# Additions of partial outputs: from VectorE to copies on ScalarE and accumulating transfers

## The chip, the cores and the metric

The kernel runs on one core of one Trainium2 chip. The metric is device microseconds of one execution. Before the change the median of three runs is 2104.79 us (2104.72 to 2105.66).

## The reference

For each of 4 batches with N = 6080 tokens and C = 256 channels, columns of q and k are normalised over the tokens, a 256x256 matrix of attention over channels is made, and v goes through it. The result, 24320 tokens in all, goes through a mixture layer with 2048 hidden columns:

```python
qn = q / (norm(q, axis=1) + 1e-06);  kn = k / (norm(k, axis=1) + 1e-06)
a = softmax(kn.transpose(0, 2, 1) @ qn / tau)
x = (v @ a).reshape(24320, 256)
h = x @ w_in
g = where(h >= 1, h, where(h <= -1, 0, (h + 1) ** 2 / 4))
out = g @ w_out
```

## The kernel before

The attention matrix is multiplied into w_in first, so that each batch has its own weights W = a @ w_in and the tokens of v meet W alone. Tokens run along the free dimension. A pair (`pairs`, index k) is two blocks of 512 tokens (480 in the last pair); a batch has 6 pairs. The 2048 hidden columns are 8 slices of 256 (index i). One group is (b, k, i); there are 4 x 6 x 8 = 192.

`h_ops` makes the four 128-row tiles of h of one group with seven products instead of eight (`strassen`, L1132), each product three matmuls of single-precision parts (`mm3`). ScalarE and VectorE turn a tile into g: saturation at L1327, square at L1331, maximum at L1336, and `operand` (L1339) splits g into a high part (L1346) and a low part (L1349). `o_ops` multiplies these by w_out into four output banks, O00 to O11, that are held for a whole pair.

For the first SPLIT[b][k] slices of a pair the output is made by `strassen_o` instead, with seven products per slice. There some products go to a bank directly, and sums of g (`combos`, L1394) go through the bank O01 in stages; ENDS gives how many stages a pair has (one for SPLIT 2 to 4, two for 5 and 6). SPLIT has 2, 2, 3, 4, 5, 5 for the pairs of the first batch, 5 throughout the next two, and 5, 5, 5, 5, 6, 6 for the last. Between stages the helper `into` reads the bank: the first time ScalarE copies it into a page in SBUF (L1438), and later times VectorE adds it to that page (L1440). At the end of a pair the four banks are read: where a page of partial sums exists VectorE adds the bank to it (L1484), and otherwise ScalarE copies the bank (L1487). SyncE then stores the page to DRAM (L1490).

The order of all work is made in Python before the program is built. `Order.op` records an operation with its engine, a cost, what it reads and writes, and a rank from the table ORDER, one number per operation; `Order.run` places the operations one after another, by rank among those that can start. It books engine times by `COST`, gives pages and banks out of pools, and for a transfer books its landing by AHEAD = 1.2, BYTES = 403e3, 1.3 us and a slack (STORE = 1.5 for stores to DRAM). Each engine then runs its own list in that order and waits on semaphores. SyncE begins the loads and stores: weights of the next groups (`load_W`, L824, two buffers in w_mem), tokens (L1265), stores (L1490). GpSimd begins loads that cast on the way (`cast_load`, L830) and does some of the subtractions.

Pages are 40 tiles of 128x512 words, those of kinds u, s, m and r among 28 of them. A page is free again when all that reads it is done.

Of the kernel before, what the change touches and what calls it, by code (L numbers as in the profile page):

```python
# [13 lines left out]
ALU = mybir.AluOpType  # L14
# [47 lines left out]
class Order:  # L62
# [20 lines left out]
    def cost(self, eng, dur, r):  # L83

        if isinstance(dur, float):
            return dur, dur, eng in self.OTHER
        kind, n, more = dur
        if kind == "dma":
            return 0.56, 0.56, False
        bank = any(x.pool and x.pool.bank for x in r)  # L90
        a, b, c = self.COST["actb" if kind == "act" and bank else kind]
        t = a + b * n + more
        return t, t + c, eng == "POOL" or eng == "DVE" and (kind == "dve1" or not bank)
# [166 lines left out]
def dve_us(n):  # L260
    return "dve", n, 0.0
# [29 lines left out]
STORE = 1.5  # L291
WOP_DUE = -48
GRAM_END = -1
CAST = 1.0
AT_ONCE = 4
# [385 lines left out]
def channel_attention_moe(ctx: ExitStack, tc: tile.TileContext, kq, kqT, vT, tau, w_in, w_out, outT):  # L681
# [132 lines left out]
    def page(kind):  # L814
        return Buf(pools["pg"], kind=kind)
# [569 lines left out]
    def combos(g, u):  # L1385
# [5 lines left out]
        for k_, out, a, c in ((0, c1, u[1, 1], u[1, 0]), (1, u[1, 0], u[1, 0], u[0, 0]), (2, c0, u[1, 1], u[1, 0]),  # L1391
# [7 lines left out]
            else:  # L1399
                op("POOL", pool_us(n), less(nc.gpsimd), r=[a, c], w=[out], due=due,  # L1400
                   other=[("DVE", dve_us(n), less(nc.vector), LATE["alt"][3])])

    def strassen_o(g):

        b, k, i = groups[g]
# [249 lines left out]
```

## Time and profile before

| | |
|---|---|
| median of three runs | 2104.79 us |
| the profiled execution | 2105.08 us |
| its span, first to last instruction | 2103.3 us |
| TensorE busy | 2090.9 us (99%) |
| VectorE busy | 1985.0 us (94%) |
| ScalarE busy | 1822.2 us (87%) |
| GpSimd busy | 896.6 us (43%) |
| granted TensorE clock | 1.00 |

Busy time is the union of the times in which an engine's instructions run. Ends of matmuls are modelled and overlap the next matmul's start, so a short idle time of TensorE is not drawn, and the steps between starts tell more.

### The profile page before, as it was taken

The numbers are of one execution on the slowest core, as the hardware profiler recorded it, in microseconds if no ns is written. First come the engines' busy times: TensorE is split into PE (matmuls) and PEld (weight loads), VectorE is DVE, ScalarE is ACT, GpSimd is POOL, SyncE is SP. The second block draws the span as 40 slices with busy tenths as digits, with TensorE's granted clock in tenths as the row PEclk, the third lists the DMA queues.
The fourth block names the chain that finished last, engine by engine and source line by source line (L and its number), as shares of the span: only waits on it lengthen the run. The fifth ranks groups of instructions, "written<-read, shape, count | busy, mean of one in ns | idle before, by whom it ended". The sixth has DMA issues, their size and how long they took to land. (4 is left out here: it accounts for less than half of the span.)

```text
span 2103.3 us, 30498 instructions
## 1 busy us (share of the span) xinstructions
PE 2090.9 (99%) x9535; PEld 1728.1 (82%) x9535; DVE 1985.0 (94%) x3165; ACT 1822.2 (87%) x3362; POOL 896.6 (43%) x953
## 2 busy tenths in 40 slices
PE   9999999999999999999999999999999999999999
PEld 7888888888878888888888888888788888788887
DVE  8898899999999999999999999999999999999998
ACT  6788889888898988888998888888999988988986
POOL 0234244544344655443435444544344443544442
PEclk9999999999999999999999999999999999999999
DMA  9865566654876866758657676675775434433432
GB/s 387 322 208 187 188 218 224 202 170 139 277 240 230 272 216 228 263 175 283 208 193 251 218 256 228 222 250 186 243 237 176 158 108 132 152 123 115 152 108 72
DMA packets 163202, 432.12 MB, mean 205 GB/s; under 512 B 22048, under 2 KB 59296, under 8 KB 160480
## 3 DMA queue, kind: packets, MB, share of 16 engines
q1 hardware_dynamic: 137744, 384.36, 52.7%
q0 software_dynamic: 25296, 45.82, 7.7%
q8 instruction: 75, 1.23, 0.2%
q14 instruction: 87, 0.71, 0.1%
HBM read 359.33 MB, written 70.78 MB: 204 GB/s over the span
## 5 line engine op out<-in xcount | busy, mean ns | idle before, releaser
L955 PE MATMUL bank<-v,w_mem 128*128 128x512 f32 (+1 forms) x3264 | 859.8, 391 | 5.1 <-DMA w_mem<-w_d 2.1
L955 PEld LDWEIGHTS bank<-v,w_mem 128*128 128x128 f32 x3264 | 603.8, 188 | 145.6 <-DVE bank L1139 8.4
L955 PE MATMUL bank<-p,wout 128*128 128x512 f32 (+1 forms) x1746 | 553.2, 388 | 0.4 <-DVE p L1349 0.4
L955 PE MATMUL bank<-x,wout 128*128 128x512 f32 (+1 forms) x1500 | 493.9, 388 | 0.0
L955 PEld LDWEIGHTS bank<-p,wout 128*128 128x128 f32 x1746 | 327.0, 188 | 67.8 <-DVE p L1349 1.3
L955 PEld LDWEIGHTS bank<-x,wout 128*128 128x128 f32 x1500 | 280.8, 188 | 57.6 <-DVE x L1349 0.5
L955 PE MATMUL bank<-x,w_mem 128*128 128x512 f32 (+1 forms) x768 | 214.8, 389 | 0.1
L955 PE MATMUL bank<-p,wsum 128*128 128x512 f32 (+1 forms) x579 | 190.1, 389 | 0.0
L955 PEld LDWEIGHTS bank<-x,w_mem 128*128 128x128 f32 x768 | 142.5, 188 | 32.0 <-ACT bank L1136 1.5
L1331 ACT ACTIVATE u_mem<-u_mem 128x512 f32<-128x512 f32 (+1 forms) x249 | 156.1, 630 | 3.5
L955 PE MATMUL bank<-x,wsum 128*128 128x512 f32 (+1 forms) x444 | 150.3, 388 | 0.0
L1331 ACT ACTIVATE p<-p 128x512 f32<-128x512 f32 (+1 forms) x229 | 144.0, 631 | 2.1
L1327 ACT ACTIVATE u_mem<-bank 128x512 f32<-128x512 f32 (+1 forms) x193 | 114.1, 592 | 29.1 <-PE bank L955 27.9
L955 PEld LDWEIGHTS bank<-p,wsum 128*128 128x128 f32 x579 | 108.0, 188 | 23.9 <-DVE p L1440 0.7
L1136 ACT COPY bank<-bank 128x512 f32<-128x512 f32 (+1 forms) x198 | 115.7, 585 | 4.6 <-PE bank L955 1.9
L1327 ACT ACTIVATE p<-bank 128x512 f32<-128x512 f32 (+1 forms) x175 | 103.1, 591 | 12.6 <-PE bank L955 11.5
L1287 DVE TENSOR_TENSOR v<-raw_mem,v 128x512 fp32r<-128x512 f32 (+1 forms) x136 | 103.6, 770 | 1.5 <-ACT v L1292 0.6
L1275 POOL TENSOR_TENSOR raw_mem<-raw_mem 128x512 f32<-128x512 f32 (+1 forms) x52 | 66.8, 1285 | 87.4 <-DVE p L1349 20.0
L1346 ACT CAST p<-p 128x512 fp32r<-128x512 f32 (+1 forms) x147 | 89.6, 614 | 13.4 <-DVE p L1336 8.1
L955 PEld LDWEIGHTS bank<-x,wsum 128*128 128x128 f32 x444 | 82.9, 188 | 17.4 <-DVE x L1349 0.4
L1336 DVE TENSOR_TENSOR u_mem<-bank,u_mem 128x512 f32<-128x512 f32 (+1 forms) x130 | 87.7, 675 | 6.3 <-ACT u_mem L1331 5.8
L1336 DVE TENSOR_TENSOR p<-bank,p 128x512 f32<-128x512 f32 (+1 forms) x133 | 89.5, 673 | 3.7 <-ACT p L1331 3.5
(519 smaller groups left out, 4619.5 us busy)
## 6 DMA issues: line engine op xcount, KB each, us to landing
w_mem<-w_d SPq DMA_DIRECT2D x176, 896.0 KB, 4.8
raw_mem<-kqT SPq DMA_DIRECT2D x60, 512.0 KB, 6.3
raw_mem<-kq SPq DMA_DIRECT2D x51, 512.0 KB, 5.8
kq<-kq SPq DMA_DIRECT2D x20, 1024.0 KB, 9.0
raw_mem<-vT SPq DMA_DIRECT2D x40, 512.0 KB, 6.6
p<-kq POOLq DMA_DIRECT2D x59, 256.0 KB, 5.8
w_d<-w_mem SPq DMA_DIRECT2D x16, 896.0 KB, 5.3
p<-wop_d SPq DMA_DIRECT2D x54, 256.0 KB, 5.2
```

The costliest lines, as they stand in the source:

```text
L955: nc.tensor.matmul(out, lhsT=lhs(a), rhs=rhs(c), start=start and m == 0, stop=stop and m == 2, skip_group_check=skip)
L1136: op("ACT", act_us(n), lambda: nc.scalar.copy(a.ap[:, :n], z.ap[:, :n]), r=[z], w=[a], due=early[1])
L1275: return lambda: e.tensor_tensor(out=part(o), in0=part(a), in1=part(c), op=ALU.subtract)
L1287: op("DVE", dve_us(n), lambda: nc.vector.tensor_tensor(out=vs[x].ap[:, 1, :n], in0=part(src), in1=f32(vs[x].ap[:, 0, :n]), op=ALU.subtract ...
L1327: op("ACT", act_us(n), lambda: nc.scalar.activation(u.ap[:, :n], h.ap[:, :n], IDENTITY_SAT240, scale=240.0), r=[h], w=[u], table="sat", du ...
L1331: op("ACT", act_us(n), lambda: nc.scalar.activation(u.ap[:, :n], u.ap[:, :n], AF.Square, bias=0.5, scale=1.0 / 480.0), r=[u], w=[u], due=due)
L1336: op("DVE", dve_us(n), lambda: nc.vector.tensor_tensor(out=out.ap[:, :n], in0=h.ap[:, :n], in1=u.ap[:, :n], op=ALU.max), r=[h, u], w=[out] ...
L1346: return lambda: f(t[0].ap[:, :n], src.ap[:, :n])
```

## The change

A new helper `add_out` stands where VectorE added a bank to a page, in `into` and at the end of a pair. Except in the very last pair, ScalarE copies the bank into a page of its own, and GpSimd begins a transfer that adds this page to the page of partial sums. Such a transfer is booked at 0.56 + 0.34 us on GpSimd in the order, and its landing with the slack STORE. ORDER has 168 more entries (11290 for 11122) and other numbers throughout.

```diff
         if kind == "dma":
-            return 0.56, 0.56, False
+            return 0.56 + more, 0.56 + more, False
...
 CAST = 1.0
+ADD = "dma", 0, 0.34
 AT_ONCE = 4
...
 ORDER = """
...
+    def add_out(bk, src, r, n, due):
+
+        if bk == (B - 1, KP - 1):
+            op("DVE", dve_us(n), lambda: nc.vector.tensor_tensor(
+                out=r.ap[:, :n], in0=src.ap[:, :n], in1=r.ap[:, :n], op=ALU.add), r=[src, r], w=[r], due=due)
+            return
+        t = page("r")
+        op("ACT", act_us(n), lambda: nc.scalar.copy(t.ap[:, :n], src.ap[:, :n]), r=[src], w=[t], due=due)
+        op("POOL", ADD, lambda: nc.gpsimd.dma_start(out=r.ap[:, :n], in_=t.ap[:, :n], accum_op=ALU.add), r=[t, r], w=[r],
+           due=due + 2, size=n * 512, slack=STORE)
+
     def strassen_o(g):
...
             else:
-                op("DVE", dve_us(n), lambda: nc.vector.tensor_tensor(
-                    out=r[x].ap[:, :n], in0=src.ap[:, :n], in1=r[x].ap[:, :n], op=ALU.add), r=[src, r[x]], w=[r[x]], due=due)
+                add_out((b, k), src, r[x], n, due)
...
                     if r:
-                        op("DVE", dve_us(n), lambda o=o, yb=yb: nc.vector.tensor_tensor(
-                           out=yb.ap[:, :n], in0=o.ap[:, :n], in1=yb.ap[:, :n], op=ALU.add), r=[o, yb], w=[yb], due=due)
+                        add_out((b, k), o, yb, n, due)
```

## Rows read from the trace of the kernel before

**Rows 1.** The page, part 1: busy us, share of the span, instructions.

```profile
PE 2090.9 (99%) x9535; PEld 1728.1 (82%) x9535; DVE 1985.0 (94%) x3165; ACT 1822.2 (87%) x3362; POOL 896.6 (43%) x953
```

**Rows 2.** Windows: length, busy us of PE, PEld, DVE, ACT, POOL; clock; DMA share; GB/s.

```profile
0.00:100.00 100.00, 97.26 (x453) 82.71 (x454) 83.28 (x128) 67.12 (x99) 11.27 (x26) 1.00 0.93 363
...
600.00:700.00 100.00, 97.78 (x462) 79.83 (x461) 96.90 (x153) 89.59 (x165) 48.44 (x61) 1.00 0.75 249
...
sum 2100.00, PE 2090.94 PEld 1728.09 DVE 1984.98 ACT 1822.22 POOL 896.55; mean PE 99.57 PEld 82.29 DVE 94.52 ACT 86.77 POOL 42.69
```

**Rows 3.** Timeline of TensorE: start, us, what, count [idle before <- releaser].

```profile
1843.29 2.88 PE L955 MATMUL bank<-v,w_mem 128*128 128x512 f32 x12
```

**Rows 4.** Timeline of TensorE: first, largest and last stalls from 100 us on.

```profile
359.64 1.63 PE L955 MATMUL bank<-v,w_mem 128*128 128x512 f32 x6 [1.04 <-DMA w_mem<-w_d]
...
626.12 0.96 PE L955 MATMUL bank<-v,w_mem 128*128 128x512 f32 x3 [1.62 <-DVE bank L1139]
...
1742.78 0.93 PE L955 MATMUL bank<-v,w_mem 128*128 128x512 f32 x3 [0.74 <-DMA w_mem<-w_d]
...
1837.03 0.97 PE L955 MATMUL bank<-v,w_mem 128*128 128x512 f32 x3
```

**Rows 5.** Waits of weight loads: who waited for whom: us, times, longest.

```profile
PEld bank L955 <- DVE bank L1139: 9.7, 27, 2.0
PEld bank L955 <- ACT bank L1136: 6.2, 20, 0.8
```

**Rows 6.** Lines L1440, L1484, L1438: ns min/median/max, first and last start, forms.

```profile
L1440 DVE TENSOR_TENSOR p<-bank,p x33: 637/676/692, 118.3 to 2080.7; 128x512 f32<-128x512 f32 x24, 128x480 f32<-128x480 f32 x9
...
L1484 DVE TENSOR_TENSOR p<-bank,p x39: 641/676/692, 184.5 to 2098.1; 128x512 f32<-128x512 f32 x32, 128x480 f32<-128x480 f32 x7
...
L1438 ACT COPY p<-bank x39: 539/579/618, 99.9 to 2054.5; 128x512 f32<-128x512 f32 x32, 128x480 f32<-128x480 f32 x7
```

**Rows 7.** Timeline of VectorE before the stall at 626.12.

```profile
607.43 0.65 DVE L1484 TENSOR_TENSOR p<-bank,p 128x480 f32<-128x480 f32 x1
...
624.78 0.68 DVE L1394 TENSOR_TENSOR p<-c,u_mem 128x512 f32<-128x512 f32 x1
625.38 0.68 DVE L1139 TENSOR_TENSOR bank<-bank,p 128x512 f32<-128x512 f32 x1
```

**Rows 8.** Timeline of ScalarE in the same stretch.

```profile
622.19 0.59 ACT L1136 COPY bank<-bank 128x512 f32<-128x512 f32 x1
622.70 0.60 ACT L1327 ACTIVATE mh_mem<-bank 128x512 f32<-128x512 f32 x1
```

**Rows 9.** Line L830: ns min/median/max of the issues, and their landings.

```profile
L830 POOL DMA_DIRECT2D p<-kq x62: 514/547/577, 148.0 to 1409.3; - x62
...
DMA to landing us min/median/max: 2.7/5.9/13.2
```

**Rows 10.** The page, part 5: busy us, mean ns of one | idle before, releaser.

```profile
L1275 POOL TENSOR_TENSOR raw_mem<-raw_mem 128x512 f32<-128x512 f32 (+1 forms) x52 | 66.8, 1285 | 87.4 <-DVE p L1349 20.0
```

**Rows 11.** DMA: queue with packets, MB, share; issues with KB, us to landing.

```profile
q0 software_dynamic: 25296, 45.82, 7.7%
...
w_mem<-w_d SPq DMA_DIRECT2D x176, 896.0 KB, 4.8
...
outT<-u_mem SPq DMA_DIRECT2D x21, 256.0 KB, 2.1
```

**Rows 12.** Timeline of SyncE: start and length of the issues.

```profile
181.38 0.32 SPq L824 DMA_DIRECT2D w_mem<-w_d  x1
...
1733.86 0.33 SPq L1490 DMA_DIRECT2D outT<-p  x1
1734.29 0.69 SPq L824 DMA_DIRECT2D w_mem<-w_d  x1
...
2044.11 0.33 SPq L824 DMA_DIRECT2D w_mem<-w_d  x1
```

**Rows 13.** Waits of SyncE: us in total, times, longest.

```profile
SPq L1490 <- DVE p L1484: 133.3, 36, 9.6
```

609 rows, old and new, of the table ORDER are left out of this document.

## The prediction

> **What bounds the kernel now.** I read the page's first part, then the windows of 100 us, the timeline of TensorE, the waits, and last the two lines that change and the queues around them. TensorE is the bound: 2090.9 of 2103.3 us busy, against 1985.0 for VectorE, 1822.2 for ScalarE and 896.6 for GpSimd [rows 1]. The windows tell how little is left. Their sum has TensorE busy 2090.94 of 2100 us, and the first window alone lacks 2.74, so 6.3 us of visible idle time lie behind it; window 600:700 holds a third of that, 2.2, with VectorE at 96.9 [rows 2]. Twelve unbroken matmuls take 2.88 us and one is drawn 0.39 long [rows 3], so the pace is (2.88 - 0.39) / 11 = 0.226 us a matmul, and each drawn idle time is a loss larger by 0.39 - 0.226 = 0.165.
>
> From 100 us on I count 22 steps of the TensorE timeline that exceed the pace by over 0.13 us, from the one that ends at 359.64 to the one that ends at 1837.03 [rows 4]. 6.3 + 22 x 0.165 = 9.9, less about 0.6 behind the last matmul, and the steps themselves give 9.2. By what ended them: VectorE 13 times, 5.0 us, of which 1.8 at 626.12 alone; weights from DRAM 3 times, 2.6 us; ScalarE 6 times, 1.5 us. The waits of weight loads show the same makers in the same order, partly hidden in the queue: VectorE's L1139 9.7 us, ScalarE's L1136 6.2 [rows 5]. So 9.2 us, 0.44% of the time, is what any relief of VectorE or ScalarE can bring; all else is matmuls that the change leaves alone. The granted clock is 1.00, the upper level of 2.4 GHz, in every window.
>
> **What it removes.** The additions of L1440 and L1484 take 0.68 us each [rows 6]. By SPLIT and ENDS a pair of one stage has 4 of them and a pair of two stages 8; 4 pairs are of the first kind and 20 of the second, 176 in all, and the last pair's 8 stay, so 168 go. VectorE's starts stand 0.60 us apart where it runs unbroken (624.78 to 625.38) [rows 7], so it gets back 168 x 0.60 = 101 us; its busy time falls to about 1884.
>
> What that is worth is read where TensorE stood. Behind 10 of the 13 stalls that VectorE ended, its unbroken run (no gap over 0.15 us) contains one or more of the additions; the largest, at 626.12, follows a run that has L1484 at 607.43 in it and four additions in all [rows 4, 7]: 4 x 0.60 = 2.4 us earlier against 1.8 us of stall. These ten sum to 3.8 us. I take -3.8; the ends are 0 (the order of after puts other work into the place) and -5.0 (all thirteen go).
>
> **What it adds to ScalarE.** 168 copies out of a bank of 0.58 us, as L1438 makes them already, with the next start 0.51 behind a copy in an unbroken run [rows 6, 8]. 168 x 0.51 = 86 us, so ScalarE goes from 1822 to 1908, and its idle time from 281 to 195. That idle time is the cover; where it is gone, copies at L1136 and squares come later, and TensorE waits for both. The six ScalarE stalls, 1.5 us, grow in my estimate as idle time shrinks: x 281/195, +0.7. Ends: -1.5 (better placed), and +5.3, if each new copy costs TensorE as much as each of the 198 at L1136 makes weight loads wait: 6.2 / 198 x 168.
>
> The bank itself comes free from a copy instead of an addition, 0.58 for 0.68 us: no cost, unless the copy stands late in ScalarE's order.
>
> **What it adds to GpSimd.** 168 issues. The nearest are the cast loads at L830: 514 to 577 ns in their largest group [rows 9]. None there accumulates; the code itself books 0.90 for one. So 168 x 0.55 = 92 us, with ends of 86 (0.514) and 216 (1.285, GpSimd's full subtraction [rows 10]): 896.6 becomes 983 to 1113 of 2103. Its idle time hides this. But each issue waits in GpSimd's order for ScalarE's copy, and on a page with two additions for the landing of the first; behind it stand L1349's and L1394's operands, which TensorE needs. I take 0 for that, since over 980 us stay idle, and price its failure below.
>
> **What it adds to the transfers.** 168 of at most 256 KB are 43 MB, about what queue 0 moves now in 7.7% of the engines' time [rows 11]: +7%, or +14% if reading the sum's own page counts as much again. In window 600:700 the engines are at 75% [rows 2], so they don't become the bound.
>
> **What it moves: the stores.** A store to outT now waits for an addition of 0.68 us; afterwards it waits for copy, issue and landing. SyncE takes its queue in order, so what stands behind a waiting store waits with it. 33 of the 96 stores have the next weights, 896 KB, as the next issue, the first at 181.38 and the last at 2044.11 [rows 12]. The trace has the price of one: a store went out at 1733.86, the weights behind it at 1734.29, and TensorE stood 0.74 (a loss of 0.9) at 1742.78 [rows 4, 12]. For final additions on pages p alone SyncE waited 133.3 us in 36 waits [rows 13], which cost nothing else that TensorE shows.
>
> The landing is unknown. From below, stores on SyncE take 2.1 us; from above, cast loads that GpSimd begins 5.9 us at the median and 13.2 at most, though these read DRAM [rows 9, 11]. The store would be later by 0.58 + 0.55 + 2.1 - 0.68 = 2.6 us up to 0.58 + 5.9 - 0.68 = 5.8. The program's own order allows for it: it books 1.2 + 262144/403000 + 1.3 + 1.5 = 4.65 us from issue to landing, and sets stores and weights by that. Between 2.1 and 5.9 I take about 4.5, since nothing is read from DRAM, and so one further stall like that at 1742.78: +1.0. Ends: -0.9 (that stall goes) and 33 x (5.9 - 4.65) = +41.
>
> The Trainium skill (DMA: Bandwidth & Descriptors, Anatomy of one DMA) puts a transfer from GpSimd at 2.0 us plus its bytes at 436 GB/s, an estimate of 2.6 us here; by that no store would be late and the sum would be 1.0 lower. The cast loads' 5.9 for the same size disagree, so I don't rest on it.
>
> **Sum.** The profiled execution took 2105.08 us. 2105.1 - 3.8 + 0.7 + 1.0 = 2103.0. It stood 0.3 above the median of 2104.79, so against that: 2102.7. Head and tail don't move: the first addition stands at 118.3 [rows 6], and the last pair keeps VectorE.
>
> **Rivals.** *All stalls shrink.* With VectorE at 1884 and ScalarE at 1908 instead of 1985 and 1822, neither is near its limit, and a new order can cure stalls that no addition stood before. Two thirds of 9.2 us: -6.1, 2098.7. For it: every stall but three is VectorE's or ScalarE's. Against: the weights' 2.6 us have nothing to do with them.
>
> *Weights behind late stores, the other side.* If a landing takes 5.9 us, it comes 1.25 after what the order books, and each of the 33 weight loads behind a store slips by that. Weights need 4.8 us [rows 11] of the 10.4 that a group lasts ((2103.3 - 100) / 192), so not all slips cost; a third gives 33/3 x 1.25 = +14: 2117 with the other terms. It decides from a landing of about 4.65 us on. For it: the cast loads' median and the stall at 1742.78. Against: stores land in 2.1 to 3.3.
>
> *GpSimd falls behind.* Its issues wait for copies and landings, or for VectorE, and operands behind them come late. If each costs its queue VectorE's 0.68 us, 168 x 0.68 = 114 us, and a tenth reaches TensorE: +11, 2114. Against it: the issues stand at 514 to 577 ns while VectorE is 94% busy [rows 1, 9]. The Trainium skill (SBUF — State Buffer, SBUF: two separate sides) says that GpSimd can't write descriptors while VectorE runs in a mode that takes the shared port, and that such a transfer looks blocked until VectorE's end; by it this rival would be the likely one. The issue times here don't show it, the landings up to 13.2 may.
>
> **Chances.** A measurement of this kernel can tell about 0.2%, 4.2 us, from no change. My forecast 0.41 (0.02 beyond 4.2 us on either side), all stalls shrink 0.33, late stores 0.20, GpSimd behind 0.06. Faster 0.33 + 0.02 = 0.35; same 0.37; slower 0.20 + 0.06 + 0.02 = 0.28. The range goes from 2094, just below all of the 9.2 us gone with nothing paid, to 2119, the late stores at a little more than my price; the forecast's own is 2099 to 2107.
>
> **What would show it.** VectorE near 1884 and ScalarE near 1908; the stall of 1.8 us gone; GpSimd's issues at 0.5 to 0.9; landings under 4.7; SyncE's stores waiting for transfers and TensorE's waits for w_mem no more than 4 us. I am wrong if TensorE's waits for w_mem pass 10 us, if ScalarE ends more than 5 us of its stalls, or if its idle time falls below 5 us, where the first rival holds.

## The result: 2132.5 us, and where the time went

The changed kernel takes 2132.48 us (median of three, 2131.14 to 2134.93) against 2104.79: a ratio of 1.013, 95% interval 1.0116 to 1.0144. It is slower by 27.7 us, outside the range of the prediction. In some executions of e1, e5 and e9 TensorE ran at the lower of its two clock levels for all or part of the time, and every ratio here leaves those out.

The page of the changed kernel, part 1, answers to [rows 1]:

```profile
PE 2099.5 (99%) x9535; PEld 1726.6 (81%) x9535; DVE 1974.4 (93%) x3123; ACT 1871.2 (88%) x3487; POOL 948.2 (45%) x1038
```

As many matmuls, in a span of 2130.7 us. VectorE's busy time was to fall by 101 us and fell by 10.6; it runs 42 instructions fewer, though 168 are gone. So 126 others came to it: counted over the trace, 59 low parts of `operand` that GpSimd made before, 45 casts that ScalarE made, 11 subtractions of tokens, and a few more. ScalarE's busy time rose by 49 us and not 86; 48 casts of `operand` left it.

Windows of the changed kernel (columns as in [rows 2]): TensorE's loss is spread over the middle of the run, and the transfers show in the DMA share, 0.75 before and 0.82 now in window 600:700.

```profile
600.00:700.00 100.00, 95.79 (x438) 75.82 (x438) 97.95 (x152) 88.14 (x164) 53.83 (x72) 1.00 0.82 257
...
1000.00:1100.00 100.00, 94.44 (x413) 76.29 (x412) 90.24 (x150) 88.93 (x174) 43.92 (x61) 1.00 0.74 217
...
1500.00:1600.00 100.00, 97.92 (x425) 79.78 (x424) 90.62 (x150) 89.73 (x173) 44.11 (x54) 0.98 0.81 248
...
sum 2100.00, PE 2072.68 PEld 1703.63 DVE 1953.03 ACT 1856.52 POOL 941.46; mean PE 98.70 PEld 81.13 DVE 93.00 ACT 88.41 POOL 44.83
```

Counted as in the prediction (steps over 0.13 us above the pace, from 100 us on), TensorE has 72 such steps of 35.5 us in place of 24 of 9.6 (the 22 of 9.2 and two that nothing names). VectorE ends 31 of them (16.0 us, 5.0 before), ScalarE 23 (9.9, 1.5 before), loads from DRAM 5 (6.8, 2.6 before) and GpSimd 2 (0.6). At the other 11 (2.2 us) the profile names no wait; eight of them are slow matmuls behind one long stall, of which the last section tells. The waits of weight loads, which answer to [rows 5]:

```profile
PEld bank L961 <- DVE bank L1145: 11.6, 32, 1.0
PEld bank L961 <- ACT bank L1142: 10.4, 22, 1.0
PEld bank L961 <- DVE p L1149: 6.5, 13, 2.5
PEld bank L961 <- DVE x L1355: 6.0, 12, 1.4
```

The new transfers (line L1417: issue ns min/median/max; then their landings, from the start of the issue) against the cast loads of [rows 9]:

```profile
L1417 POOL DMA_DIRECT2D p<-u_mem x24: 852/880/1147, 189.9 to 2067.1; - x24
...
DMA to landing us min/median/max: 3.2/5.1/9.3
```

GpSimd issues one in 0.88 us, near the 0.90 that the order books, and not in the 0.55 of a cast load. A landing takes 5.1 us at the median where the order books 4.65. The Trainium skill (DMA: Bandwidth & Descriptors, Anatomy of one DMA) would put it at an estimate of 2.6 us; the shortest of 168 took 3.2.

Queue 0 and the weights, which answer to [rows 11]: the engines' time for queue 0 rises by 11.6 points, between the 7 and the 14 that the prediction named, and weights land 0.9 us later.

```profile
q0 software_dynamic: 49488, 89.48, 19.3%
...
w_mem<-w_d SPq DMA_DIRECT2D x176, 896.0 KB, 5.7
```

Two stalls show how a landing reaches TensorE. The first is in the chain of the work that ended last (start, length, what): the transfer that reads the copy in page c lands at 363.18, only then is the page free for ScalarE's saturation L1333, the copy L1416 behind it comes late, and TensorE, which needs the bank, starts again at 364.91 after 1.46 us.

```profile
355.27 0.89 POOL u_mem L1417
356.16 0.06 issue
356.22 6.96 DMA y_mem<-c
...
363.26 0.07 ACT c L1333
...
364.28 0.59 ACT u_mem L1416
364.86 0.04 issue
364.91 1.19 PE bank L961 x4
```

The second is read from four timelines of the changed kernel, GpSimd, ScalarE, VectorE and TensorE, in this order. A transfer into y_mem begins at 1546.79. The next one into the same page has to wait for its landing, and GpSimd stands 2.62 us until 1554.63. Behind it in GpSimd's order are sums that ScalarE's L1209 needs (2.75 us idle), VectorE's L1207 waits for that (2.13), and L1149 behind it on VectorE is what TensorE waits for (2.08).

```profile
1546.79 1.11 POOL L1417 DMA_DIRECT2D y_mem<-mh_mem  x1
...
1554.63 0.87 POOL L1417 DMA_DIRECT2D y_mem<-p  x1 [2.62 <-issue]
1555.25 1.16 POOL L1229 TENSOR_TENSOR raw_mem<-raw_mem 128x128 f32<-128x128 f32 x2
```

```profile
1556.03 1.55 ACT L1209 CAST p<-raw_mem 128x384 fp32r<-128x384 f32 x3 [2.75 <-POOL raw_mem L1229]
```

```profile
1556.57 0.56 DVE L1207 TENSOR_TENSOR p<-raw_mem,p 128x384 fp32r<-128x384 f32 x1 [2.13 <-ACT p L1209]
1557.09 0.69 DVE L1207 TENSOR_TENSOR x<-raw_mem,p 128x512 fp32r<-128x512 f32 x1
1557.70 0.68 DVE L1149 TENSOR_TENSOR p<-bank,p 128x512 f32<-128x512 f32 x1
```

```profile
1558.44 1.04 PE L961 MATMUL bank<-v,w_mem 128*128 128x512 f32 x3 [2.08 <-DVE p L1149]
1559.27 0.63 PE L961 MATMUL bank<-x,wout 128*128 128x512 f32 x1
1559.70 0.63 PE L961 MATMUL bank<-p,wout 128*128 128x512 f32 x1
...
1563.12 0.40 PE L961 MATMUL bank<-p,wout 128*128 128x512 f32 x1
1563.35 0.39 PE L961 MATMUL bank<-x,wout 128*128 128x512 f32 x1
```

### The profile page after: what moved, and what is told of

It is laid out like the page before. It is cut to its first block, busy times and chain, and to the rows that moved or that the text cites. A ratio compares the mean times of both kernels' runs of the same rounds, so it can differ in the third digit from the quotient of the medians.

```text
span 2130.7 us, 30958 instructions
## 1 busy us (share of the span) xinstructions
PE 2099.5 (99%) x9535; PEld 1726.6 (81%) x9535; DVE 1974.4 (93%) x3123; ACT 1871.2 (88%) x3487; POOL 948.2 (45%) x1038
## 3 DMA queue, kind: packets, MB, share of 16 engines
q0 software_dynamic: 49488, 89.48, 19.3%
## 4 chain that ended last, share of the span: by engine, by line
PE 71%; DVE 15%; DMA 5%; ACT 5%; issue 3%; POOL 1%; SPq 0%; DVEq 0%; POOLq 0%; ACTq 0%
PE bank L961 68%; DVE p L1355 2%; PE bank L1537 2%; DVE x L1355 2%; DVE p L1400 1%; DMA w_mem<-w_d 1%; DVE p L1342 1%; DVE bank L1145 1%; DMA kq<-kq 1%; DVE u_mem L1342 1%; ACT p L1352 1%; DVE u_mem L1400 1%; DVE x L973 1%; DVE bank L1342 1%; DMA raw_mem<-kqT 0%
## 5 line engine op out<-in xcount | busy, mean ns | idle before, releaser
L961 PE MATMUL bank<-x,w_mem 128*128 128x512 f32 (+1 forms) x792 | 221.7, 390 | 0.7 <-DVE bank L1145 0.4
L961 PE MATMUL bank<-p,wsum 128*128 128x512 f32 (+1 forms) x549 | 177.2, 390 | 2.5 <-ACT u_mem L1416 1.5
L1337 ACT ACTIVATE p<-p 128x512 f32<-128x512 f32 (+1 forms) x253 | 158.7, 631 | 2.1
L1333 ACT ACTIVATE u_mem<-bank 128x512 f32<-128x512 f32 (+1 forms) x180 | 106.4, 592 | 24.3 <-PE bank L961 23.0
L961 PEld LDWEIGHTS bank<-p,wsum 128*128 128x128 f32 x549 | 102.4, 188 | 26.5 <-ACT u_mem L1416 2.4
L1333 ACT ACTIVATE p<-bank 128x512 f32<-128x512 f32 (+1 forms) x187 | 110.8, 593 | 14.4 <-PE bank L961 13.7
L1293 DVE TENSOR_TENSOR v<-raw_mem,v 128x512 fp32r<-128x512 f32 (+1 forms) x135 | 110.5, 824 | 2.6 <-POOL v L1301 1.5
L961 PEld LDWEIGHTS bank<-x,wsum 128*128 128x128 f32 x474 | 88.6, 188 | 20.7 <-ACT y_mem L1455 1.7
L1229 POOL TENSOR_TENSOR raw_mem<-raw_mem 128x128 f32<-128x128 f32 x96 | 45.7, 487 | 106.4 <-DVE p L1355 35.1
```

What stands on the lines that cost most here:

```text
L961: nc.tensor.matmul(out, lhsT=lhs(a), rhs=rhs(c), start=start and m == 0, stop=stop and m == 2, skip_group_check=skip)
L1229: op(eng, pool_us(128) if eng == "POOL" else dve_us(128), lambda d=d, a=a, c=c, o=o, v=v: v.tensor_tensor(out=eight(f)[:, d, :], in0=eight ...
L1293: op("DVE", dve_us(n), lambda: nc.vector.tensor_tensor(out=vs[x].ap[:, 1, :n], in0=part(src), in1=f32(vs[x].ap[:, 0, :n]), op=ALU.subtract ...
L1333: op("ACT", act_us(n), lambda: nc.scalar.activation(u.ap[:, :n], h.ap[:, :n], IDENTITY_SAT240, scale=240.0), r=[h], w=[u], table="sat", du ...
L1337: op("ACT", act_us(n), lambda: nc.scalar.activation(u.ap[:, :n], u.ap[:, :n], AF.Square, bias=0.5, scale=1.0 / 480.0), r=[u], w=[u], due=due)
```

## Experiments

Each ratio is against the kernel before on the same chip, with its 95% interval; multiplied with 2104.8 us it gives the differences named here. Most runs change only what an instruction does, and keep the order that the program plans for the changed kernel; e7 and e8 keep the order of the kernel before in the same way, and e4 is planned anew. An interval reaches 2 to 4 us to either side, so a difference of that size between two runs is uncertain. Where a sum or part of it is missing, the times stand for kernels that leave that work out.

**e1, no transfer.**

```diff
-        op("POOL", ADD, lambda: nc.gpsimd.dma_start(out=r.ap[:, :n], in_=t.ap[:, :n], accum_op=ALU.add), r=[t, r], w=[r],
+        op("POOL", ADD, lambda: None, r=[t, r], w=[r],
```

> The changed kernel in its own order, with ScalarE's 168 copies, but GpSimd begins no accumulating transfer (the second half of each of these sums is left out). Theory 1, the transfers: they land later than the 4.65 us that the order books, and pages and stores that wait for them hold up ScalarE, SyncE and the weights; then the time comes back to 2104 to 2110. Theory 2, GpSimd's queue: 168 issues of 0.9 us and their waits for copies delay the operands behind them; it also gives 2104 to 2110, and e2 and e3 tell it from theory 1. Theory 3, the order and ScalarE's load (copies of 86 us, and work that went from GpSimd and ScalarE to VectorE): the time stays at 2122 or more.

2108.8 us, 1.0023 (1.0014 to 1.0033). 22.5 us of the 27.4 go with the transfers; +4.8 us stay with the order and the copies. Theory 3 falls as the main cause.

**e2, short transfers.**

```diff
-... nc.gpsimd.dma_start(out=r.ap[:, :n], in_=t.ap[:, :n], accum_op=ALU.add) ...
+... nc.gpsimd.dma_start(out=r.ap[:, :16], in_=t.ap[:, :16], accum_op=ALU.add) ...
```

> The changed kernel with each accumulating transfer cut to 16 of its 512 columns (the rest of the sum is left out): as many issues, rows and waits, 1/32 of the bytes. Theory 1, by the bytes: landings fall below 4.65 us and the time to 2104 to 2112. Theory 2, GpSimd's queue: issues stay at 0.88 us and the time stays at 2125 or more. Theory 3: 2125 or more.

2116.4 us, 1.0057 (1.0042 to 1.0072). The issue stays at 0.89 us and landings fall to 3.1: the time lies between the two expectations. More than half of the loss hangs on the bytes, the rest does not.

**e3, plain transfers of the same bytes.**

```diff
-... nc.gpsimd.dma_start(out=r.ap[:, :n], in_=t.ap[:, :n], accum_op=ALU.add) ...
+... nc.gpsimd.dma_start(out=r.ap[:, :n], in_=t.ap[:, :n]) ...
```

> The changed kernel with a plain transfer in place of each accumulating one (the page of sums is overwritten, not added to). Theory 1: if the reading of the sum's page is what makes it late, landings fall by 1 us or more and the time to 2110 to 2120; if any transfer of 256 KB lands so late, the time stays within 5 us of 2132. Theory 2: the issue falls from 0.88 to about 0.55 us, GpSimd gets back some 55 us, and the time falls by 5 us or more with landings unchanged. Theory 3: within 3 us of 2132.

2110.3 us, 1.0029 (1.0017 to 1.004): 1.3 us over e1, which the intervals can't tell from nothing. Line L1417 and queue 0 of this kernel:

```profile
L1417 POOL DMA_DIRECT2D p<-u_mem x24: 536/554/588, 190.7 to 2044.5; - x24
...
DMA to landing us min/median/max: 2.2/3.2/8.3
```

```profile
q0 software_dynamic: 38352, 89.48, 13.0%
```

It is not 168 transfers of 256 KB through GpSimd that cost, but that they accumulate. Order, copies, waits and bytes are those of the changed kernel, and 21.3 us are gone. Without accumulation the issue falls from 0.88 to 0.55 us, the landing from 5.1 to 3.2, and the packets of the new transfers from 24192 to 13056 (each less the 25296 of before). Their share of the engines' time falls from 11.6 points to 5.3.

**e4, the ranks of before.** The change is made in the kernel before, with RANK from the old list; copy and transfer use the rank of the addition that they replace.

```diff
-        o.due = dict.fromkeys(o.alts, RANK[len(self.ops)])
+        at = len(self.ops) - self.extra
+        if dur is ADD:
+            at, self.extra = at - 1, self.extra + 1
+        o.due = dict.fromkeys(o.alts, RANK[at])
...
```

> The changed kernel with the ranks of the order before the change: copy and transfer take the rank of the addition that they replace, all other operations their old one. Theory 3 in the form that the new ORDER numbers are to blame: 2105 to 2115. Theories 1 and 2: the change itself costs, so the time stays at 2120 or more, and more than 2132 if the new numbers had been fitted to it.

2178.5 us, 1.0352 (1.0337 to 1.0368). The new numbers as a whole are not to blame: with the change made, they win 47 us over the old ones. Here too the plan gives VectorE other work: it runs 3155 instructions, 158 more than the 2997 that are left without the 168 additions.

**e5 and e9, stores that don't wait.** In the stores of the moved sums:

```diff
-                        out=outT[ct * P:(ct + 1) * P, c0:c0 + n], in_=yb.ap[:, :n]), r=[yb], due=due + 1,
+                        out=outT[ct * P:(ct + 1) * P, c0:c0 + n], in_=src_of(yb, r)), r=[yb], due=due + 1,
```

where `src_of` gives wout[:, 0, 0] for the moved sums, a page long ready.

> The changed kernel in its own order, but the stores to outT of the moved sums read a page that is long ready (part of wout; what is stored is not the sum), so SyncE no longer waits for accumulating transfers. Their number, bytes and issues stay. Theory 1a, late landings reach TensorE through SyncE's queue and the weights behind the stores: the time falls from 2132 by 10 us or more, to 2122 or less, and TensorE's waits for w_mem from 5.3 to under 3. Theory 1b, they reach it through pages that are held until the landing, and theory 2, through GpSimd's queue: 2128 or more.

> The kernel of e5 again, whose executions fell on a chip that granted TensorE less clock (0.70 and 1.2 GHz in two of four), so that they can't be compared. Theory 1a, late landings reach TensorE through SyncE's queue: 2122 or less. Otherwise 2128 or more.

e5 gave 1.0159 (1.0138 to 1.0181) from two executions, and e9 2134.3 us, 1.0141 (1.0124 to 1.0158) from three. Theory 1a falls: with the stores free nothing is won. The trace of the changed kernel agrees: SyncE's waits ahead of stores fell from 329 us in 91 waits to 289 in 78, 245 of them for landings.

**e6, a fixed source.**

```diff
-... nc.gpsimd.dma_start(out=r.ap[:, :n], in_=t.ap[:, :n], accum_op=ALU.add) ...
+... nc.gpsimd.dma_start(out=r.ap[:, :n], in_=f32(wout[:, 0, 0].rearrange("p x c -> p (x c)"))[:, :n], accum_op=ALU.add) ...
```

> The changed kernel in its own order, but the accumulating transfer reads a page that is long ready (part of wout; other values are added) instead of ScalarE's copy: the copy's page is free at once, and GpSimd doesn't wait for the copy. Stores still wait for the landing. Theory 1b, pages held until the landing: the time falls by 10 us or more, to 2122 or less. Theory 2, GpSimd's waits for copies: it falls too, by 5 us or more, with GpSimd's waits for L1416 gone. Theory 1a, the stores: 2128 or more.

2128.1 us, 1.0108 (1.0093 to 1.0124): 4.6 us less than the changed kernel, where theory 1b expected 10 or more and theory 2 expected 5 or more. Pages of copies held until the landing, and GpSimd's waits for copies, cost about that much together; the two intervals still touch.

**e7, no addition in the kernel before.**

```diff
                 op("DVE", dve_us(n), lambda: nc.vector.tensor_tensor(
-                    out=r[x].ap[:, :n], in0=src.ap[:, :n], in1=r[x].ap[:, :n], op=ALU.add), r=[src, r[x]], w=[r[x]], due=due)
+                    out=r[x].ap[:, :n], in0=src.ap[:, :n], in1=r[x].ap[:, :n], op=ALU.add) if (b, k) == (B - 1, KP - 1) else None,
+                   r=[src, r[x]], w=[r[x]], due=due)
```

and the same at L1484.

> The kernel before, in its own order, with the same 168 additions left out and nothing in their place (that part of the sums is missing): VectorE's relief alone. The prediction's first term: 3.8 us less than before, at most 5.0, so 2099.5 to 2101.5. If the relief is worth more than the stalls show: under 2099. If it is worth nothing, because other waits end last there: within 1 us of before.

2100.2 us, 0.9978 (0.9969 to 0.9988): -4.6, as the first term of the sum said (-3.8, at most -5.0). In that order this is all that could be won, had the additions vanished without any price.

```profile
PE 2086.8 (99%) x9535; PEld 1730.7 (82%) x9535; DVE 1924.7 (92%) x2997; ACT 1822.5 (87%) x3362; POOL 906.4 (43%) x953
```

VectorE's busy time falls by 60 us and not by 101. Added up by line, its other instructions are drawn some 30 us longer, 14.6 of them at L1349; why was not followed.

**e8, a copy for each addition, in the kernel before's order.**

```diff
                         op("DVE", dve_us(n), lambda o=o, yb=yb: nc.vector.tensor_tensor(
-                           out=yb.ap[:, :n], in0=o.ap[:, :n], in1=yb.ap[:, :n], op=ALU.add), r=[o, yb], w=[yb], due=due)
+                           out=yb.ap[:, :n], in0=o.ap[:, :n], in1=yb.ap[:, :n], op=ALU.add) if (b, k) == (B - 1, KP - 1) else nc.scalar.copy(yb.ap[:, :n], o.ap[:, :n]),
+                           r=[o, yb], w=[yb], due=due)
```

and the same at L1440.

> The kernel before, in its own order, with a copy by ScalarE into the page in the place of each of the 168 additions by VectorE, and no transfer (the page is overwritten, not added to). The prediction's first two terms: -3.8 + 0.7 us, 2101 to 2103. Theory 3, ScalarE's 86 us more are what costs: 2106 or more.

2125.7 us, 1.0096 (1.0079 to 1.0113), as theory 3 expected. Against e7 the copies cost 25 us here. This order books nothing for them on ScalarE, so it shows what copies cost that come unplanned, not what they cost in the changed kernel; e14 does that.

**e10, free stores and a fixed source.** The edits of e5 and e6 together.

> The changed kernel in its own order with e5's stores (from a page long ready) and e6's source (a page long ready) together: no store waits for a landing, no copy's page is held by one, GpSimd doesn't wait for copies. What is left of the accumulating transfers: their issues, their bytes on the DMA engines, and the page of sums, which its next user gets only after the landing. Theory 1, late landings through stores and copies' pages: 2115 or less. Theory 4, the transfers' load on the DMA engines and GpSimd's issues: 2122 or more.

2125.9 us, 1.0104 (1.0087 to 1.012): with neither stores nor copies' pages waiting for a landing, 5.5 us come back of 27.4, as theory 4 expected. Theory 1 as the main cause falls, but for the page of sums, whose next user still waits.

**e11, nobody waits.**

```diff
+    spare = [dram.tile([P, TB], F32, name=f"spare{i}") for i in range(8)]
+    turn = iter(range(1000))
...
-... nc.gpsimd.dma_start(out=r.ap[:, :n], in_=t.ap[:, :n], accum_op=ALU.add) ...
+... nc.gpsimd.dma_start(out=spare[next(turn) % 8][:, :n], in_=f32(wout[:, 0, 0].rearrange("p x c -> p (x c)"))[:, :n], accum_op=ALU.add) ...
```

> The changed kernel in its own order, but the 168 accumulating transfers read a page long ready and add to 8 spare tiles in DRAM, so that no page, no store and no engine but GpSimd has to do with them (the sums are left out). Issues and bytes stay. Theory 1, landings: 2110 to 2116, GpSimd's issue alone being left. Theory 4, load on the DMA engines: 2122 or more.

2123.4 us, 1.0088 (1.0073 to 1.0103), as theory 4 expected. Accumulating transfers that no page, store or other engine has to do with still cost some 14 us over e1. They add to tiles in DRAM and not in SBUF: they land in 6.0 us at the median (5.1 in the changed kernel) and queue 0 takes 20.8% of the engines' time (19.3%), so they are near to the changed kernel's and not the same. Two places that they hit stand in VectorE's timeline of e11, first a cast load that lands late, later a row of norms from DRAM, which SyncE loads:

```profile
613.97 0.69 DVE L973 TENSOR_TENSOR x<-raw_mem,p 128x512 fp32r<-128x512 f32 x1 [1.37 <-DMA p<-kq]
614.58 0.69 DVE L1355 TENSOR_TENSOR p<-u_mem,p 128x512 fp32r<-128x512 f32 x1
...
1459.94 0.48 DVE L1056 SCALAR_TENSOR_TENSOR q<-gacc,cols,q 128x256 f32<-128x256 f32 x1 [2.10 <-DMA q<-rn_d]
```

and from TensorE's, which stands behind the operands that VectorE then makes late:

```profile
615.32 1.22 PE L961 MATMUL bank<-p,wsum 128*128 128x512 f32 x2 [2.01 <-DVE p L1355]
...
1462.61 0.96 PE L961 MATMUL bank<-v,w_mem 128*128 128x512 f32 x3 [2.14 <-DVE cols L1061]
```

These are single places. In all VectorE stands idle for landings 7.8 us in e11 and 1.7 in e12, 3.9 and 1.3 of it for cast loads, so such waits are a part of the price. And in the changed kernel they are not what VectorE waits for: it stands 1.2 us for landings in all and never for a cast load, but 86.5 us for ScalarE, 79.7 in e1 (all from 100 us on).

**e12, the issue alone.** As e11 with 16 columns, into four tiles of 128x16 in SBUF.

```diff
-... dma_start(out=spare[next(turn) % 8][:, :n], in_=...[:, :n], accum_op=ALU.add) ...
+... dma_start(out=spare[next(turn) % 4][:, :16], in_=...[:, :16], accum_op=ALU.add) ...
```

> As e11, with 16 columns into 4 spare tiles in SBUF: 168 accumulating issues and next to no bytes, and nobody waits for them. e1 without any issue took 2108.8, e2 with short transfers that copies, pages and stores wait for 2116.4. Theory 2, GpSimd's queue: 2114 to 2118, as e2. If e2's rest was landings of 3.1 us: 2108 to 2111.

2112.8 us, 1.0038 (1.0023 to 1.0053), between the two expectations. Its interval overlaps e1's, so the issues cost some 3 us or nothing that these runs tell. The bytes, e11 less e12, cost 10.5; with them the place changes too, from SBUF to DRAM. Bytes within SBUF aren't free of waits in any run: e10, which has them, lies 13.9 us over e12, the wait for the page of sums included.

**e13, the same load by SyncE.**

```diff
-        op("POOL", ADD, lambda: nc.gpsimd.dma_start(out=r.ap[:, :n], in_=t.ap[:, :n], accum_op=ALU.add), r=[t, r], w=[r],
+        op("POOL", ADD, lambda: [nc.sync.dma_start(out=spare[next(turn) % 32][:, :n], in_=f32(wout[:, 0, 0].rearrange(
+            "p x c -> p (x c)"))[:, :n]) for _ in range(2)][0], r=[t, r], w=[r],
```

> The changed kernel in its own order without accumulating transfers (e1), but SyncE begins in the place of each two plain transfers of 256 KB from a page long ready to spare tiles in DRAM, which nobody waits for: about the time on the DMA engines that an accumulating transfer takes, on SyncE's queue instead of GpSimd's, and no issue on GpSimd. e1 took 2108.8, e12 2112.8, e11 2123.4. Theory 4, load on the DMA engines wherever it comes from: 2115 or more. Theory 5, the accumulating transfers stand in GpSimd's own queue ahead of the cast loads that VectorE needs: 2108 to 2112.

2114.1 us, 1.0041 (1.0026 to 1.0056), between the two expectations. The transfers go to 32 spare tiles in DRAM. Queue 1 of this kernel takes 12.8 points more of the engines' time than before:

```profile
q1 hardware_dynamic: 186128, 471.67, 65.5%
```

That load, about the accumulating transfers', costs 3.8 us over e1 by the ratios, and the intervals overlap. The trace also puts three waits of GpSimd, 10.5 us, down to landings of these transfers, so they are not quite without anyone who waits. By these ratios the load on the engines explains a part of e11's bytes at most. Cast loads land in 6.1 us at the median in e1, 6.5 in e13 and 6.9 in e11. Whether the rest comes by loads that stand behind the transfers in GpSimd's queue, by the accumulation in DRAM, or by another property of such a transfer, no run separates.

**e14, no copy and no transfer.** The edit of e1, and `lambda: None` for ScalarE's copy.

> The changed kernel in its own order with neither the 168 copies nor the transfers (those parts of the sums are left out): against e1 the copies alone are missing. The prediction's term for ScalarE was +0.7: 2107.5 to 2108.8. If the 86 us of copies are what e1 still loses: 2104 or less. If the order loses it, with its 126 operations more on VectorE: 2107 or more.

2106.1 us, 1.0006 (0.9997 to 1.0016), between the expectations. Against e1 the copies cost 3.6 us. Without additions, copies and transfers the new order takes as long as the kernel before with its additions. With the same additions gone the old order stands at 0.9978 (e7): so the new order gives back the 5.9 us between the two. That the 126 operations moved to VectorE do it is read from their number and was not tried by itself.

## Why the prediction was wrong

The step that failed is "What it adds to the transfers": I priced the 168 transfers at 0, since the DMA engines would not be full, and took them for transfers like the others. They are what lost the time. Without them 22.5 us come back (e1), and as plain transfers of the same bytes they cost 1.3 (e3).

The ledger, each step a difference of ratios times 2104.8 us: the changed order with neither copies nor transfers +1.3 (e14), copies +3.6 (e1), issues +3.2, not clear of noise (e12), bytes +10.5 (e11, in DRAM), everything that waits for a landing +8.8 (the changed kernel). Sum 27.4. Only of the last two steps do the intervals on either side not touch.

1. *VectorE's relief, -3.8.* The size was right: -4.6 in e7. But it did not arrive: the new order gives back 5.9 us (e14 against e7), by my reading through the 126 operations that came to VectorE. The order books each issue on GpSimd at 0.90 us, 151 us in all, and the program gives GpSimd's low parts and ScalarE's casts a second engine; that these bookings are why they moved is my reading. I named "other work in the place" as the end of 0 and did not look for what would be moved; L1349 and L1346 have the alternatives in the code.
2. *ScalarE, +0.7.* It was 3.6, inside the bounds I had kept. But the stalls that ScalarE ends grew from 1.5 to 9.9 us, past the 5 that I had set as a sign of being wrong: 5.6 in e14 without copies or transfers, 5.5 in e1 with the copies, and the rest with the transfers.
3. *GpSimd, 0.* The issue costs 0.88 us where the nearest row gave 0.55; this may be 3 us. The wait for a landing on a page with two additions, which I named and priced at 0, is the chain at 1554.63.
4. *The transfers, "they don't become the bound".* I asked whether the DMA engines would be full; in windows of 100 us behind the first their share is 0.51 to 0.88, so over such stretches they were not. At the same bytes an accumulating transfer takes 2.2 times the engines' time of a plain one (11.6 against 5.3 points), 0.33 us more to issue and 1.9 more to land. Where nobody waits for them, the bytes cost 10.5 us (e11), in part by loads that land later for VectorE. How much goes which way in the changed kernel stays open, since there VectorE hardly waits for loads itself.
5. *Late stores, +1.0, and the rival of the other side.* The landing was above 4.65 us, as that rival wanted, and the kernel came out slower; but not by the stores. No run shows the +1.0: with stores free (e9) nothing is won, and SyncE waits less for them than before. TensorE's stalls for weights rose from 2.6 to 6.0 us, under the 10 that I had set as a sign. Landings cost by pages and by GpSimd's own waits, some 4.6 us in e6, and the rest of the 8.8 is not separated further.
6. *The rival "GpSimd falls behind"* named a part of the price: GpSimd's waits for copies and landings are in the 4.6 us of e6. The issues alone cost 3.2 us or nothing (e12). The Trainium skill (SBUF — State Buffer, SBUF: two separate sides) has VectorE hold up GpSimd's descriptors while it runs in a mode that takes the shared port. That doesn't show in the issues: they take 0.85 to 1.29 us with VectorE busy 93%, and 0.89 at the median beside its casts as beside its other instructions. I called the rival likely by that page without asking which of VectorE's instructions run in such a mode.

"All stalls shrink" needed a relief that was not there: VectorE's and ScalarE's stalls grew from 6.5 to 25.9 us.

## What to carry to other kernels

Work taken off an engine by an edit comes back where a planner may place other work on it, so read which operations have a second engine before counting the relief. A transfer that accumulates is a different thing from a plain one of the same bytes: price its issue, its time on the DMA engines and its landing from a run of its own. And ask of added transfers not only whether the engines are full but who waits for their landings, and which loads beside them land later; here the stalls grew while the engines' share over 100 us stayed under 0.9.

## What was not expected of the hardware

An accumulating transfer of 256 KB within SBUF took GpSimd 0.88 us to issue and 3.2 to 9.3 to land, a plain one 0.55 and 2.2 to 8.3.

After TensorE stood 2.08 us until 1558.44 its granted clock fell: it is 0.50, the lower of its two levels (1.2 GHz), from 1559.2 to 1562.6, and matmuls stand 0.43 us apart there instead of 0.23. So this stall cost some 1.6 us (eight steps of 0.2) beyond its own length. The stall of 2.01 us at 615.32 in e11 has the same mark, a granted clock of 0.50 from 615.3 to 618.7. Not every stall of this size has it: the one that ended at 1071.5 in the changed kernel, 2.2 us over the pace, was followed by a granted clock of 1.00. What decides was not tried. From 100 us on the profiled executions of e6 and e10 have three such stretches each, the changed kernel and e11 one, and e1, e3, e12 and e13 none, so differences of 4 or 5 us between these runs hold some of that too.
